# Transposing normalised rows and key features by DMA instead of on TensorE, in a fused attention and feed-forward kernel

## Chip, core and metric

The kernel runs on one core of a Trainium2 chip. The metric is the device time of one execution in microseconds (us). The core has five engines with queues of their own: PE (TensorE; PEld is its weight load), DVE (VectorE), ACT (ScalarE), POOL (GpSimd) and SP (SyncE, which here issues every DMA). Each engine takes its instructions strictly in order, and a wait on a semaphore holds everything behind it on that engine.

## What is computed

One layer on x of 2048 rows by 1024 columns, in bf16: a segmented attention with a compressive memory, and a gated feed-forward, each behind a layer norm and with a residual.

```
xn = layernorm(x)
q, k, v = xn @ wq, xn @ wk, xn @ wv            # 32 heads of 32
phi(t) = where(t > 0, t + 1, exp(t))
for s in range(4):                             # segments of 512 rows
    a_dot = softmax(qs @ ks.T * 32**-0.5 + causal mask) @ vs
    a_mem = (phi(qs) @ M) / (phi(qs) @ z + 1e-6)
    o_s = g * a_mem + (1 - g) * a_dot          # g = sigmoid(beta), per head
    M += phi(ks).T @ vs ;  z += phi(ks).sum(rows)
h = x + concat(o_s) @ wo
hn = layernorm(h)
out = h + (silu(hn @ w1) * (hn @ w3)) @ w2     # 3584 hidden columns
```

## The kernel before

Work is described as a graph of operations, each with an engine (or a choice of two), an estimated cost, a priority class and the buffers that it reads and writes. `Graph.schedule` (L208) lays the graph out by a simulated clock of its own: whenever an engine is free, it takes the ready operation of the lowest class number. What comes out is a fixed order of instructions on each engine, and the semaphore waits that the buffers need; the chip runs that order. A DMA is given a short time on SP, its bytes at `DMA_RATE` on one shared line, and `DMA_FIX` more (L77, L78, L326 to L329). Changing one operation can so change the order of all that follows.

PE contracts over the partition dimension, so rows that are to be multiplied by a weight must first lie with their columns on the partitions. The kernel keeps such transposed tiles for each segment s: `xnT[s]` of the normalised input and `hnT[s]` of the normalised residual, both [128, 8, 512] (eight blocks of 128 columns, 512 rows). The tile `xnT[1]` lies in the buffer `hnT0`, `xnT[2]` in `hnT1`, and `xnT[3]` in the buffer of `xnT[0]` (L521).

- `ln1(s)` (L731) loads four tiles of 128 rows into `xs` (four buffers), normalises each in place (statistics on DVE, the inverse root on POOL, the scaling on DVE at L727), transposes it and puts it in `xnT[s]`.
- `qkv(s)` (L747) streams wq, wk and wv in halves of 1 MB into three `wp` buffers, and makes `qT`, `kT` and `v`, in groups of eight matmuls of 512 columns.
- `memory(s)` (L794), for segments 0 to 2, makes the key features phi(k) for two blocks of heads at a time (`pk`, two buffers), transposes them to `pkn` (two buffers), and multiplies them with v (eight matmuls of 129 columns). The product updates M and z.
- `attention(s)` (L838) runs eight units of four heads: scores (L868), three exponentials on ACT (L883), causal masks on POOL (L888), value products and sums (L921), and the division and mixing on DVE and POOL.
- `wo_stage(s)` (L963), four tiles of 128 rows each: the output projection, the residual with a reload of x (`xr`, one buffer), a store of h to a scratch tensor, the norm into `hn` (one buffer), its transpose into `hnT[s]`.
- `ffn_up` and `ffn_down` (L986, L1017) work on two blocks of 1024 rows. Block 0 uses `hnT[0]` and `hnT[1]`. The output projections of segments 2 and 3 are added between chunks of block 0.

A transpose in this kernel is one batch of eight PE instructions (`transposes`, L605, recorded at L609), each with a 128x128 block as one operand and an identity as the other. The batch claims one bank of the accumulator (PSUM), and `evac` (L616) copies the 128x1024 result to SBUF on DVE (L621) or ACT (L620), whichever the planner finds free. As long as attention runs, dense work has two of the eight banks, 6 and 7 (`dense_group`, L583); afterwards it has them all. Dense matmuls are recorded at L597.

Of the kernel before, what the change touches and what calls it, by code (L numbers as in the profile page):

```python
# [69 lines left out]
class Graph:  # L70
# [126 lines left out]
    def dma(self, out, in_, cls=5, deps=(), eng="sp"):  # L197
        n = 1
        for s in out.shape:
            n *= s  # L200
        o = self.op("sp", 60.0, None, reads=(in_,), writes=(out,), cls=cls, deps=deps,
                    kind="dma")
        o.emit = lambda e, g: [e.dma_start(out, in_)]
        o.bytes = n * SIZE[out.dtype]
        return o


# [244 lines left out]
def dve_ns(n, mode=1):  # L452
    return 150.0 + n / (0.96 * mode)
# [10 lines left out]
class Kernel:  # L464
# [266 lines left out]
    def ln1(self, s):  # L731
        for i in range(4):
            t = 4 * s + i
            x = self.xs[t % 4][:, :]
            self.g.dma(x, self.x2d[t * 128:(t + 1) * 128, :], cls=0 if s == 0 else 2)
            if t == 1:
                self.ln_act(t, x, x)
            else:
                self.ln(t, x, x, 2 if s == 0 else 5)
            gr = self.dense_group() if s else Group([(6,), (7,), (4,), (5,)], safe=True)  # L740
            self.transposes(gr, [(c * 128, self.xs[t % 4][:, c * 128:(c + 1) * 128])
                                 for c in range(8)], 2 if s == 0 else 4)
            out = self.xnT[s][:, :, i * 128:(i + 1) * 128]
            self.evac(gr, out, 1024, lambda b: b.rearrange("p (k n) -> p k n", k=8), cls=1,
                      bf=True)
# [48 lines left out]
    def memory(self, s):  # L794

        p = s % 2
        v = self.v[p]
        for pr in range(4):
            pk = self.pk[pr % 2]
            self.phi(self.kT[p][:, 2 * pr:2 * pr + 2, :], pk[:, :, :], 4)  # L800
            gr = self.dense_group()
            self.transposes(gr, [((a * 4 + kc) * 128, pk[:, a, kc * 128:(kc + 1) * 128])
                                 for a in range(2) for kc in range(4)], 4)
            pkn = self.pkn[pr % 2]
            self.evac(gr, pkn[:, :, :], 1024, lambda b: b.rearrange("p (k n) -> p k n", k=8),
                      cls=3, bf=True)
            gr = self.dense_group()
            items = []
            for a in range(2):
                for kc in range(4):  # L810
                    items.append((lambda gr, a=a: self.bank(gr, 0, 129, 132 * a),
                                  pkn[:, a * 4 + kc, :], v[:, kc, 2 * pr + a, 0:129],
                                  kc == 0, kc == 3, 129))
            self.mms(gr, items, 4, split=8)
            acc = self.Macc[:, 2 * pr:2 * pr + 2, :]

            def upd(e, gr, acc=acc):
                ps = self.bank(gr, 0, 264).rearrange("p (a n) -> p a n", a=2)[:, :, 0:129]
                if s == 0:
                    return [e.tensor_copy(acc, ps)]  # L820
                return [e.tensor_tensor(acc, acc, ps, op=ALU.add)]

            self.g.op("dve", dve_ns(258), upd, reads=[acc] if s else [], writes=[acc], cls=3,
                      group=gr)
            Mb = self.Mbf[p][:, 2 * pr:2 * pr + 2, :]
            am = self.Macc[:, 2 * pr:2 * pr + 2, 0:128]
            bl = self.blk[:, :].unsqueeze(1).to_broadcast([128, 2, 128])
            self.either(lambda e, Mb=Mb, am=am, bl=bl: e.tensor_tensor(Mb, am, bl, op=ALU.mult),
                        256, 2, [am, self.blk[:, :]], [Mb], 4)
            for a in range(2):  # L830
                zs = self.zsel[p][:, 2 * pr + a, :].rearrange(
                    "p (j n) -> p j n", j=4)[:, :, 1:2].rearrange("p j n -> p (j n)")
                z = self.Macc[:, 2 * pr + a, 128:129]
                hm = self.hmask[:, :]
                self.pool_op(lambda e, zs=zs, z=z, hm=hm: e.tensor_scalar(
                    zs, hm, z, None, op0=ALU.mult), 4, [hm, z], [zs], 4)
# [126 lines left out]
    def wo_stage(self, s):  # L963
        oT = self.oT[s % 2]
        for i in range(4):
            t = 4 * s + i
            xr, h, hn = self.xr[0], self.h[t % 2], self.hn[0]
            self.g.dma(xr[:, :], self.x2d[t * 128:(t + 1) * 128, :], cls=2)
            for half in range(2):
                gr = self.dense_group(s >= 2)  # L970
                self.mms(gr, [(lambda gr: self.bank(gr), oT[:, c, i * 128:(i + 1) * 128],
                               self.wo[:, c, half * 512:(half + 1) * 512], c == 0, c == 7, 512)
                              for c in range(8)], 5 if s < 2 else 7)
                hs = h[:, half * 512:(half + 1) * 512]
                xs = xr[:, half * 512:(half + 1) * 512]
                self.g.op("dve", dve_ns(512), lambda e, gr, hs=hs, xs=xs: [e.tensor_tensor(  # L976
                    hs, xs, self.bank(gr), op=ALU.add)], reads=[xs], writes=[hs], cls=3,
                    group=gr)
            self.g.dma(self.hd[t * 128:(t + 1) * 128, :], h[:, :], cls=3)
            self.ln(16 + t, h[:, :], hn[:, :], 4)  # L980
            gr = self.dense_group(s >= 2)
            self.transposes(gr, [(c * 128, hn[:, c * 128:(c + 1) * 128]) for c in range(8)], 3)
            self.evac(gr, self.hnT[s][:, :, i * 128:(i + 1) * 128], 1024,
                      lambda b: b.rearrange("p (k n) -> p k n", k=8), cls=3, bf=True)

    def ffn_up(self, blk, ch):  # L986
        n = self.n_w13
# [139 lines left out]
```

## Time and profile before

| | |
|---|---|
| time, median of 3 runs | 946.5 us (945.31 to 946.81) |
| the profiled execution, its own time | 944.8 us |
| its span, first to last instruction | 943.1 us |
| PE busy | 915.6 us, 97% |
| DVE busy | 434.7 us, 46% |
| ACT busy | 321.6 us, 34% |
| POOL busy | 172.8 us, 18% |
| moved by DMA | 85.83 MB, 91 GB/s on average |

The profile is one execution, recorded instruction by instruction. A group of instructions is named by its line, engine, operation, and what it writes and reads (`pkn<-ps` writes pkn from the accumulator). "Idle before, releaser" is time in which an engine stood ahead of such an instruction, and the instruction whose end freed it. Matmul ends are modelled, so starts are the better measure of how long one takes.

### The profile page before, as it was taken

Reading aid. Unit: us, or ns where it says so; the run is one execution under the profiler, and the core shown is the slowest. Engines: PE = TensorE matmul, PEld = TensorE weight load, DVE = VectorE, ACT = ScalarE, POOL = GpSimd, SP = SyncE. Lnnn points to the kernel's source line nnn. Section 1 sums busy time; section 2 is a strip of 40 time slices with the busy share of each in tenths; the row PEclk is TensorE's granted clock in tenths of the full one; section 3 lists DMA queues with packets and bytes.
Section 4 is the critical chain, followed back from the end, with each engine's and each line's share of the span. In section 5 each row is a group of like instructions: output and inputs, shape, how many; then the busy total and the mean of one; then the engine's idle time right before and its main releaser. Section 6 shows DMA issues by size and latency. Waiting matters only on the chain.

```text
span 943.1 us, 13518 instructions
## 1 busy us (share of the span) xinstructions
PE 915.6 (97%) x5661; PEld 421.3 (45%) x5760; DVE 434.7 (46%) x749; ACT 321.6 (34%) x360; POOL 172.8 (18%) x274
## 2 busy tenths in 40 slices
PE   7999999998999999999999999999999999999998
PEld 3444344443444444444444444444444444444443
DVE  3895638768766766544544321211333343331101
ACT  4877638787677771121121110000111111110000
POOL 2563313563644552000000000000000000000000
PEclk9999999999999999999999999999999999999999
DMA  9532343222331318433343221011332123300110
GB/s 313 190 117 71 105 141 106 90 90 70 112 101 35 91 45 293 129 114 90 101 145 90 73 62 45 28 40 45 90 91 71 50 63 90 90 17 29 45 45 29
DMA packets 103005, 85.83 MB, mean 91 GB/s; under 512 B 3104, under 2 KB 90144, under 8 KB 102944
## 3 DMA queue, kind: packets, MB, share of 16 engines
q1 hardware_dynamic: 102944, 84.95, 29.5%
q8 instruction: 46, 0.75, 0.3%
q14 instruction: 15, 0.12, 0.0%
HBM read 76.55 MB, written 8.39 MB: 90 GB/s over the span
## 4 chain that ended last, share of the span: by engine, by line
PE 94%; ACT 2%; DVE 2%; issue 1%; DMA 1%; SPq 0%; DVEq 0%; ACTq 0%
PE ps L597 86%; PE ps L921 4%; PE ps L868 3%; PE ps L609 1%; DMA xr<-in_A_x_dram 1%; DVE h L976 1%; ACT eB L883 0%; DMA xs<-in_A_x_dram 0%; ACT eA L883 0%; DVE lnst L718 0%; ACT xnT L620 0%; ACT v L620 0%; DVE v L621 0%; ACT qT L620 0%; ACT pkn L620 0%
## 5 line engine op out<-in xcount | busy, mean ns | idle before, releaser
L597 PE MATMUL ps<-hnT,w1b 128*128 128x512 bf16 x875 | 221.0, 379 | 1.4 <-issue 0.3
L597 PE MATMUL ps<-hnT,w3b 128*128 128x512 bf16 x875 | 220.2, 379 | 2.0 <-issue 0.6
L1005 ACT ACTIVATE sg<-ps 128x512 bf16<-128x512 f32 x112 | 66.9, 597 | 407.6 <-PE ps L597 400.4
L597 PE MATMUL ps<-w2b,hm 128*128 128x512 bf16 x880 | 195.5, 379 | 0.8
L1008 DVE SCALAR_TENSOR_TENSOR t<-sg,ps 128x512 bf16<-128x512 bf16 x112 | 76.9, 686 | 158.5 <-ACT sg L1005 158.4
L597 PEld LDWEIGHTS ps<-w2b,hm 128*128 128x128 bf16 x896 | 87.7, 98 | 105.7
L597 PEld LDWEIGHTS ps<-hnT,w3b 128*128 128x128 bf16 x896 | 87.0, 98 | 105.4 <-issue 1.6
L597 PEld LDWEIGHTS ps<-hnT,w1b 128*128 128x128 bf16 x896 | 86.7, 98 | 104.1 <-issue 6.2
L1013 DVE SCALAR_TENSOR_TENSOR hm<-t,ps 128x512 bf16<-128x512 bf16 x112 | 76.9, 686 | 81.1 <-PE ps L597 79.2
L1035 DVE TENSOR_TENSOR ob<-hr,ps 128x512 bf16<-128x512 bf16 x32 | 22.0, 687 | 143.4 <-PE ps L597 143.4
L883 ACT ACTIVATE eA<-ps 128x2048 bf16<-128x2048 f32 x32 | 60.0, 1876 | 15.8 <-PE ps L868 9.4
L597 PE MATMUL ps<-xnT,wp 128*128 128x512 bf16 x244 | 58.4, 379 | 2.9 <-issue 1.6
L597 PE MATMUL ps<-hnT,wp 128*128 128x512 bf16 x246 | 59.1, 380 | 1.4 <-issue 1.3
L597 PE MATMUL ps<-wo,oT 128*128 128x512 bf16 x248 | 58.8, 379 | 1.4 <-DVE h L976 0.6
L888 POOL TENSOR_SCALAR_AFFINE_SELECT eC<-eC 128x512 bf16<-128x512 bf16 x64 | 41.0, 662 | 41.7 <-ACT eC L883 41.7
L883 ACT ACTIVATE eC<-ps 128x1536 bf16<-128x1536 f32 x32 | 46.4, 1450 | 6.2 <-PE ps L868 6.1
L883 ACT ACTIVATE eB<-ps 128x1536 bf16<-128x1536 f32 x32 | 46.3, 1447 | 5.9 <-PE ps L868 5.9
L932 DVE STREAM_TRANSPOSE T<-ps 128x512 f32<-128x512 f32 x32 | 22.9, 716 | 37.0 <-PE ps L921 37.0
L888 POOL TENSOR_SCALAR_AFFINE_SELECT eA<-eA 128x512 bf16<-128x512 bf16 x32 | 21.4, 670 | 89.1 <-ACT eA L883 89.1
L868 PE MATMUL ps<-qT,kT 32*128 32x256 bf16 (+3 forms) x512 | 34.5, 302 | 3.0 <-ACT eB L883 1.2
L597 PEld LDWEIGHTS ps<-wo,oT 128*128 128x128 bf16 x256 | 24.0, 98 | 29.0 <-issue 0.9
L597 PEld LDWEIGHTS ps<-xnT,wp 128*128 128x128 bf16 x256 | 23.1, 98 | 28.5 <-issue 3.7
(108 smaller groups left out, 795.7 us busy)
## 6 DMA issues: line engine op xcount, KB each, us to landing
w1b<-in_B_w_dram SPq DMA_DIRECT2D x28, 512.0 KB, 3.9
w3b<-in_B_w_dram SPq DMA_DIRECT2D x28, 512.0 KB, 3.8
wp<-in_A_wk_dram SPq DMA_DIRECT2D x8, 1024.0 KB, 5.4
wp<-in_A_wv_dram SPq DMA_DIRECT2D x8, 1024.0 KB, 6.0
wp<-in_A_wq_dram SPq DMA_DIRECT2D x7, 1024.0 KB, 5.2
w2b<-in_B_w_dram SPq DMA_DIRECT2D x7, 1024.0 KB, 8.0
xs<-in_A_x_dram SPq DMA_DIRECT2D x16, 256.0 KB, 3.7
xr<-in_A_x_dram SPq DMA_DIRECT2D x16, 256.0 KB, 2.9
```

What stands on the lines that cost most here:

```text
L597: return [e.matmul(p[0](gr), p[1], p[2], start=p[3], stop=p[4]) for p in part]
L609: return [e.transpose(b[:, c:c + 128], s, self.ident[:, :]) for c, s in items]
L868: ins.append(e.matmul(self.bank(gr, j, n, off), k[r, g, 128 * kc:128 * kc + 128], q[r, g, 128 * kc:512], start=True, stop=True, tile_posit ...
L883: return [e.activation(et[:, :, :], src, AF.Exp, scale=self.scale)]
L888: self.pool_op(lambda e, m=m: e.affine_select(m, m, pattern=[[0, 4], [1, 128]], compare_op=ALU.is_ge, fill=0.0, base=0, channel_multiplier ...
L921: ins.append(e.matmul(self.ps[r, b * 512 + 128 * kc:(b + 1) * 512], lhsT, src[:, j, :], start=first, stop=True, tile_position=(0, 32 * j), ...
L932: G.op("dve", dve_ns(512), lambda e, gr: [e.transpose(T1, self.bank(gr))], writes=[T1], cls=0, group=gd)
L976: self.g.op("dve", dve_ns(512), lambda e, gr, hs=hs, xs=xs: [e.tensor_tensor(hs, xs, self.bank(gr), op=ALU.add)], reads=[xs], writes=[hs], ...
L1005: self.g.op("act", act_ns(512), lambda e, gr, sg=sg: [e.activation(sg, self.bank(gr), AF.Tanh, scale=0.5)], writes=[sg], cls=2, group=gg)
L1008: e.scalar_tensor_tensor(t1, sg, 1.0, self.bank(gr), op0=ALU.add, op1=ALU.mult)], reads=[sg], writes=[t1], cls=2,
L1013: e.scalar_tensor_tensor(dst, t1, 0.5, self.bank(gr), op0=ALU.mult, op1=ALU.mult)], reads=[t1], writes=[dst], cls=2,
L1035: self.g.op("dve", dve_ns(512), lambda e, gr, hs=hs, ob=ob: [e.tensor_tensor(ob, hs, self.bank(gr), op=ALU.add)], reads=[hs], writes=[ob], ...
```

## The change

The transposes of three kinds of tiles are no longer made by PE. A new graph operation, `dma_t`, is one DMA on SP that reads a tile of 128 rows by 1024 columns in SBUF and writes it, transposed in blocks of 128 columns, to another place in SBUF. It claims no bank, and nothing is evacuated. It is planned with 2 x 262144 bytes.

```
+    def dma_t(self, out, in_, cls=5):
+        o = self.op("sp", 60.0, None, reads=(in_,), writes=(out,), cls=cls, kind="dma")
+        o.emit = lambda e, g: [e.dma_start_transpose(out, in_)]
+        o.bytes = 2 * 262144
+        return o
...
# ln1
-            gr = self.dense_group() if s else Group([(6,), (7,), (4,), (5,)], safe=True)
+            if s:
+                self.g.dma_t(self.xnT[s][:, :, i * 128:(i + 1) * 128], x, 3)
+                continue
+            gr = Group([(6,), (7,), (4,), (5,)], safe=True)
...
# memory
-            gr = self.dense_group()
-            self.transposes(gr, [((a * 4 + kc) * 128, pk[:, a, kc * 128:(kc + 1) * 128])
-                                 for a in range(2) for kc in range(4)], 4)
             pkn = self.pkn[pr % 2]
-            self.evac(gr, pkn[:, :, :], 1024, lambda b: b.rearrange("p (k n) -> p k n", k=8),
-                      cls=3, bf=True)
+            self.g.dma_t(pkn[:, :, :], pk[:, :, :].rearrange("p a n -> p (a n)"), 3)
...
# wo_stage
-            gr = self.dense_group(s >= 2)
-            self.transposes(gr, [(c * 128, hn[:, c * 128:(c + 1) * 128]) for c in range(8)], 3)
-            self.evac(gr, self.hnT[s][:, :, i * 128:(i + 1) * 128], 1024,
-                      lambda b: b.rearrange("p (k n) -> p k n", k=8), cls=3, bf=True)
+            self.g.dma_t(self.hnT[s][:, :, i * 128:(i + 1) * 128], hn[:, :], 2)
```

The first segment's rows stay on PE. 320 PE instructions and 40 evacuations go, and 40 DMAs come. A tile that such a DMA reads (`xs`, `pk`, `hn`) may be overwritten only when the DMA has finished. All engines' orders are laid out anew, and the lines behind the new function have other numbers (L597 is L604, L868 is L874, L921 is L927).

## The prediction

> **What bounds the kernel now.** I read the profile from the whole to the parts: busy time of each engine, the chain of work that ended last, then stretches of time, then the transposes themselves. From the first page, span, busy time and chain:
>
> ```profile
> span 943.1 us, 13518 instructions
> PE 915.6 (97%) x5661; PEld 421.3 (45%) x5760; DVE 434.7 (46%) x749; ACT 321.6 (34%) x360; POOL 172.8 (18%) x274
> PE 94%; ACT 2%; DVE 2%; issue 1%; DMA 1%; SPq 0%; DVEq 0%; ACTq 0%
> ```
>
> PE is busy for 915.6 of 943.1 us and holds 94% of the chain, so only what shortens PE's own queue, or lengthens what it waits for, can move the end. The busy time by stretches (the columns are PE, its weight loads, DVE, ACT, POOL, the granted clock, the DMA engines' share and GB/s) shows where PE is not busy:
>
> ```profile
> 0.00:15.00 15.00, 9.21 (x56) 4.59 (x58) 7.37 (x23) 6.91 (x9) 7.03 (x25) 1.00 0.91 275
> 15.00:355.00 340.00, 324.69 (x2880) 149.91 (x2922) 232.49 (x428) 244.43 (x238) 154.50 (x229) 1.00 0.33 105
> 355.00:510.00 155.00, 153.68 (x775) 72.08 (x789) 78.87 (x129) 29.12 (x44) 11.32 (x20) 1.00 0.46 138
> ```
>
> From 15 to 355 us (projections, attention, and dense work between) PE idles 15.3 us, ACT is busy for 244 of 340 us, DVE for 232, the DMA engines for a third. After 355 us PE has hardly a gap. The clock is 1.00 throughout, so no term below needs a correction for it.
>
> **What is removed on PE.** The same view for L609, the line of all transposes, PE and weight loads:
>
> ```profile
> 0.00:15.00 15.00, 2.21 (x32) 1.81 (x32) 1.00 0.91 275
> 15.00:943.00 928.00, 24.32 (x320) 19.39 (x320) 1.00 0.29 88
> ```
>
> The 32 before 15 us are the first segment's and stay. The other 320, in 40 batches of eight, go: 12 for rows of segments 1 to 3, 12 for key features, 16 for the rows after the output projection. The rows are 24.32 us busy, 0.61 us a batch, but the end of a matmul is modelled and the next one starts before it. The timeline of PE gives the step from one start to the next:
>
> ```profile
> 35.87 0.62 PE L609 MATMUL ps<-ident,pk 128*128 128x128 bf16 x8
> 36.45 0.62 PE L609 MATMUL ps<-ident,xs 128*128 128x128 bf16 x8
> 37.28 0.63 PE L597 MATMUL ps<-v,pkn 128*128 128x129 bf16 x8 [0.21 <-DVE pkn L621]
> ...
> 79.76 0.61 PE L609 MATMUL ps<-ident,pk 128*128 128x128 bf16 x8
> 80.30 0.40 PE L921 MATMUL ps<-eA,v 128*32 128x512 bf16 x4
> ...
> 103.39 0.62 PE L609 MATMUL ps<-ident,pk 128*128 128x128 bf16 x8
> 103.85 0.38 PE L597 MATMUL ps<-wp,hnT 128*128 128x512 bf16 x1
> ```
>
> The steps are 0.58 (36.45 less 35.87), 0.54 and 0.46 us; between 0.46 and 0.61 I take 0.55, nearest to the middle one. 40 x 0.55 = 22 us, with bounds 18.4 and 24.3. The chain passes through PE nearly everywhere, so this comes off the end, not only off a busy sum.
>
> **What goes with it.** A batch also holds one of two accumulator banks until it is evacuated. What PE waited for from 15 to 355 us, with the sum, the number and the longest:
>
> ```profile
> PE ps L609 <- DVE h L976: 1.4, 1, 1.4
> PE ps L609 <- DVE v L621: 0.7, 2, 0.3
> PE ps L597 <- ACT xnT L620: 0.6, 1, 0.6
> PE ps L609 <- ACT v L620: 0.5, 2, 0.2
> PE ps L597 <- DVE pkn L621: 0.2, 1, 0.2
> PE ps L597 <- ACT pkn L620: 0.2, 1, 0.2
> ```
>
> The three waits on xnT and pkn (1.0 us) go, since nothing is evacuated there. The waits of the transposes on v and h (2.6 us) were for a bank that some other matmul will now want: I count them as staying. So 1 us, between 0 and 3.6.
>
> The 40 evacuations leave ACT and DVE. The 23 and 17 of them take 1.02 and 0.69 us each by the pkn groups (ACT, DVE):
>
> ```profile
> L620 ACT ACTIVATE pkn<-ps 128x1024 bf16<-128x1024 bf16 x5 | 5.1, 1022 | 2.7 <-PE ps L609 2.7
> L621 DVE COPY pkn<-ps 128x1024 bf16<-128x1024 bf16 x7 | 4.8, 688 | 0.9 <-PE ps L609 0.6
> ```
>
> That is 23 us of ACT and 12 us of DVE, worth nothing directly, since both have a third of the stretch free; they only make late evacuations less likely.
>
> **What is added.** 40 crossbar transfers of 256 KB, issued by SP in order with the weight loads. No row shows such a transfer. The nearest are plain DMAs (KB each, us from issue to landing):
>
> ```profile
> xr<-in_A_x_dram SPq DMA_DIRECT2D x16, 256.0 KB, 2.9
> xs<-in_A_x_dram SPq DMA_DIRECT2D x16, 256.0 KB, 3.7
> wp<-in_A_wv_dram SPq DMA_DIRECT2D x8, 1024.0 KB, 6.0
> w2b<-in_B_w_dram SPq DMA_DIRECT2D x7, 1024.0 KB, 8.0
> wo<-in_A_wo_dram SPq DMA_DIRECT2D x1, 2048.0 KB, 11.6
> ```
>
> Bounds: 2.9 us, a transfer of the same size that is merely copied, and 11.6 us, the longest landing on the page. I take 4 us, near the rows of equal size, with a little for the transposing. [...]
>
> Who waits for it, in order of how soon? The tightest consumer is the memory product of key features (L597, v and pkn). PE's order there, first segment, before; pk is the key-feature tile, pkn its transpose, the L868 rows are score products:
>
> ```order
> L597 MATMUL ps<-wp_76,xnT 128x512 x12
> L868 MATMUL ps<-qT_82,kT_83 128x384 x4
> L609 MATMUL ps<-ident,pk_90 128x128 x8
> L609 MATMUL ps<-ident,xs_77 128x128 x8
> L597 MATMUL ps<-v_84,pkn_94 128x129 x8
> ```
>
> And the same place in PE's queue after (L927 is what was L921, the value products):
>
> ```order
> L604 MATMUL ps<-wp_76,xnT 128x512 x12
> L874 MATMUL ps<-qT_82,kT_83 128x384 x4
> L604 MATMUL ps<-xnT,wp_74 128x512 x12
> L874 MATMUL ps<-qT_82,kT_83 128x256 x4
> L874 MATMUL ps<-qT_82,kT_83 128x128 x4
> L927 MATMUL ps<-eA_96,v_84 32x512 x4
> ...
> L604 MATMUL ps<-xnT,wp_74 128x512 x4
> L874 MATMUL ps<-qT_82,kT_83 128x512 x4
> L604 MATMUL ps<-v_84,pkn_94 128x129 x8
> ```
>
> The product has moved back by 16 projection matmuls and one unit's value products. Their steps on PE before, and the end of the pk tile on DVE:
>
> ```profile
> 29.88 2.76 PE L597 MATMUL ps<-wp,xnT 128*128 128x512 bf16 x12
> 32.58 0.40 PE L868 MATMUL ps<-qT,kT 32*128 32x512 bf16 x4
> ...
> 38.11 0.40 PE L921 MATMUL ps<-eA,v 128*32 128x512 bf16 x4
> 39.54 0.81 PE L597 MATMUL ps<-xnT,wp 128*128 128x512 bf16 x3 [0.16 <-issue]
> ...
> 34.70 0.64 DVE L791 TENSOR_TENSOR pk<-phe,phr 128x1024 bf16<-128x1024 bf16 x1
> ```
>
> 12 matmuls step 2.70 us (32.58 less 29.88), so 16 take 3.6; the value products step 1.43 (39.54 less 38.11); two score batches, each below the 0.40 of the quoted row since ends overlap, about 0.6: 5.6 us after 35.87, so 41.5. pk is done at 35.34. That leaves 6.1 us from ready to wanted, and a landing of 4 us fits. There are 12 such places; for those where the transfer stands behind a 1 MB load I keep 2 us in all, between 0 and what the slow rival below gives.
>
> The other 28 have more room. SP's queue at the same place, before (wp are projection weights, xs rows of the input):
>
> ```order
> L203 DMA wp_75<-in_A_wk_dram 128x8x512
> L203 DMA wp_76<-in_A_wv_dram 128x8x512
> L203 DMA xs_77<-in_A_x_dram 128x1024
> L203 DMA xs_78<-in_A_x_dram 128x1024
> L203 DMA xs_79<-in_A_x_dram 128x1024
> L203 DMA xs_80<-in_A_x_dram 128x1024
> L203 DMA wp_74<-in_A_wq_dram 128x8x512
> ```
>
> And after (hnT_72 takes the transposed rows of segment 1):
>
> ```order
> L203 DMA wp_75<-in_A_wk_dram 128x8x512
> L210 DMA_TRANSPOSE pkn_94<-pk_90 128x8x128
> L203 DMA wp_76<-in_A_wv_dram 128x8x512
> L210 DMA_TRANSPOSE hnT_72<-xs_77 128x8x128
> L210 DMA_TRANSPOSE pkn_95<-pk_91 128x8x128
> L210 DMA_TRANSPOSE hnT_72<-xs_78 128x8x128
> L210 DMA_TRANSPOSE hnT_72<-xs_79 128x8x128
> L210 DMA_TRANSPOSE hnT_72<-xs_80 128x8x128
> L203 DMA xs_77<-in_A_x_dram 128x1024
> L203 DMA wp_74<-in_A_wq_dram 128x8x512
> ```
>
> Six transposes have come in between. They wait for DVE's tiles, and the load of wp_74 for segment 1 is queued behind them and behind a reload of xs_77 that needs a finished transpose. The cover is the lead of that load: issued here, first used there (SP, then PE):
>
> ```profile
> 54.48 0.38 SPq L203 DMA_DIRECT2D wp<-in_A_wq_dram  x1
> 81.73 0.59 PE L597 MATMUL ps<-hnT,wp 128*128 128x512 bf16 x2 [0.16 <-issue]
> ```
>
> 27 us ahead, with a landing of 6.0 us by the wp row: SP may be some 20 us late before PE notices. I count nothing. Without that cover each microsecond of lateness would be one of PE.
>
> Last, the single hn buffer: a new row may be written only when the transfer has read the old one, and DVE waits with its evacuations queued behind. Two hn rows before stand at:
>
> ```profile
> 142.93 0.54 DVE L727 TENSOR_SCALAR hn<-h,lnmv,rstd 128x1024 bf16<-128x1024 bf16 x1
> 146.38 0.54 DVE L727 TENSOR_SCALAR hn<-h,lnmv,rstd 128x1024 bf16<-128x1024 bf16 x1
> ```
>
> 3.45 us apart, against 4 us: at most half a microsecond of DVE, which has a third of its time free. Nothing on the path.
>
> Sum, against the profiled execution's own 944.8 us (span 943.1 and 1.7 around it): 944.8 - 22 - 1 + 2 = 923.8. The median of the runs before, 946.5, is 1.7 above that execution; a median of runs after should stand likewise, so I give 925.5. About 0.2% is what a measurement here can tell from no change, 944.6 to 948.4.
>
> **The rivals.**
>
> Forecast (0.68): as above. With the outer values of each gain, 24.3 and 3.6 instead of 22 and 1, and no new wait, it is 946.5 - 27.9 = 918.6; a denser order by the shorter evacuation queues could add some of the other idle time, a third of 15.3 us, so 913.5.
>
> The time saved turns into idle time (0.12): attention could be held by its exponentials on ACT, and PE would wait for scores instead of transposing. For it: ACT is the next busiest engine there, with 244 of 340 us. Against it: ACT has 96 us free from 15 to 355 us and loses 23 more of work, and feed-forward matmuls fill in. If half the gain is lost, 946.5 - 11 = 935.5.
>
> The crossbar lands late (0.15, slower): the eight 128-column blocks of a transfer pass one after the other, and PE stands at the 12 products of pkn. At the landing of the w2b row, 8.0 us, each lacks 2 us, 24 in all: 946.5 - 23 + 24 = 947.5; at 11.6 us each lacks 5.6, 67 in all, and it is 990. It decides from 6 + 23/12 = 7.9 us on. For it: nothing here shows 128 columns turned by a DMA, and SP puts five transfers in a row, which would then also queue. Against it: rows of equal size land in 2.9 to 3.7 us. [...]
>
> Little or no change (0.05): the two last in part, by a landing of about 7.9 us.
>
> That the change doesn't do what it says is excluded by the order: of L609's 44 batches PE keeps the first four.
>
> **The numbers.** Range 913.5 to 949: the forecast's best end, the idle rival, and the late crossbar to its near end; beyond it lie the late crossbar's long end, about 0.12, and a little below. Faster by over 0.2%: 0.68 + 0.12 = 0.80; within: 0.05; slower: 0.15.
>
> **What would show it.** Right: transposing DMAs landing in 3 to 5 us, PE busy about 892 us, idle from 15 us on about as before, no row of PE waiting on pkn over 1 us. Wrong: landings above 8 us, PE waits on pkn, hnT or wp that add up to over 10 us, or DVE waiting on hn's transfer with evacuations late behind it.

## The result and the profile after

The changed kernel takes 916.8 us (median of 4 runs, 916.1 to 919.0) against 945.9 us before: ratio 0.9697, 95% interval 0.9676 to 0.9719, some 29 us less. The forecast was 925.5 us, with a range down to 913.5.

The profiled execution took 916.63 us. Its span, busy times and chain, from the first page:

```profile
span 914.6 us, 12864 instructions
PE 895.2 (98%) x5346; PEld 402.7 (44%) x5440; DVE 431.8 (47%) x739; ACT 295.2 (32%) x330; POOL 173.5 (19%) x274
PE 95%; DVE 2%; issue 1%; ACT 1%; DMA 0%; POOL 0%; SPq 0%; ACTq 0%
```

PE is still the bound, busy for 98% of the span and with 95% of the chain. Of the 28.5 us that the span lost, PE's busy time gave 20.4 (915.6 less 895.2) and its idle time 8.1 (27.5 to 19.4). Both traces miss about as many matmul records (94 of 5440 here, 99 of 5760 before), so the difference can be used. The idle time of one trace alone is overstated: the trace of the section "What a new order is worth" below, whose order is mostly that of before, misses none of 5760 and shows 17.9 us idle in a span of 942.9. Neither it nor the other traces below that miss none (the plans with 1, 3 and 8 tiles) has a row "issue" for PE from 15 to 330 us; so such rows are holes that missing records leave, not waits. ACT lost 26 us and 30 instructions: 23 evacuations, and seven others that the new order puts on DVE.

Where the idle time went can be read from the busy time by stretches and from what PE waited for, here from 15 to 330 us:

```profile
15.00:330.00 315.00, 307.81 (x2594) 135.06 (x2632) 228.73 (x415) 221.04 (x213) 150.87 (x224) 1.00 0.53 142
```

```profile
PE ps L604 <- issue: 4.6, 29, 0.2
PE ps L604 <- DVE h L982: 0.7, 2, 0.5
PE ps L604 <- DVE qT L628: 0.4, 1, 0.4
PE ps L604 <- DVE kT L628: 0.3, 1, 0.3
PE ps L604 <- DVE T L943: 0.2, 1, 0.2
PE ps L604 <- DVE lnst L725: 0.2, 1, 0.2
```

Apart from "issue", 1.8 us of waits are left. In the trace of before the same table, over the same stretch, has 8.7 us in thirteen rows. Not only the waits on xnT and pkn are gone, but also those of the transposes on h and v, of other dense matmuls on h, and the waits on exponentials and reciprocals. Of before, beside the rows that the prediction shows:

```profile
PE ps L597 <- DVE h L976: 1.2, 2, 0.6
PE ps L868 <- ACT eA L883: 1.1, 1, 1.1
PE ps L597 <- DVE o L952: 0.9, 1, 0.9
PE ps L868 <- ACT eB L883: 0.8, 2, 0.5
PE ps L868 <- DVE Rc L941: 0.6, 1, 0.6
```

The new transfers, from the page and the list of DMA issues (KB each where known, median us from issue to landing):

```profile
q1 hardware_dynamic: 145184, 95.45, 37.9%
...
xs<-in_A_x_dram SPq DMA_DIRECT2D x16, 256.0 KB, 6.9
...
hnT<-hn SPq DMA_TRANSPOSE x16, 3.9
pkn<-pk SPq DMA_TRANSPOSE x12, 3.6
hnT<-xs SPq DMA_TRANSPOSE x8, 3.5
xnT<-xs SPq DMA_TRANSPOSE x4, 3.2
```

They land in 3.2 to 3.9 us, close to the 4 us of the forecast. The input rows, reloaded behind them in the same queue, now land in 6.9 us where they took 3.7; in the other orders below that have all 40 transfers it is between 3.5 and 6.0, so much of that is this order's.

The first memory product, whose slack the prediction worked out. SP's queue and PE's timeline (start, length):

```profile
35.58 1.34 SPq L210 DMA_TRANSPOSE pkn<-pk  x1
36.98 0.56 SPq L203 DMA_DIRECT2D wp<-in_A_wv_dram  x1
37.58 2.63 SPq L210 DMA_TRANSPOSE hnT<-xs  x1
40.26 2.71 SPq L210 DMA_TRANSPOSE pkn<-pk  x1
43.01 4.67 SPq L210 DMA_TRANSPOSE hnT<-xs  x3
47.73 0.58 SPq L203 DMA_DIRECT2D xs<-in_A_x_dram  x1
48.35 0.44 SPq L203 DMA_DIRECT2D wp<-in_A_wq_dram  x1
```

```profile
36.09 2.76 PE L604 MATMUL ps<-xnT,wp 128*128 128x512 bf16 x12
38.79 0.34 PE L874 MATMUL ps<-qT,kT 32*128 32x256 bf16 x8
...
41.56 0.63 PE L604 MATMUL ps<-v,pkn 128*128 128x129 bf16 x8
```

The product starts at 41.56, without a wait in front of it (41.5 was worked out), 6 us after SP issued its transfer. The five transfers that SP issues from 37.58 on hold it for some 10 us, yet the load of wq behind them leaves at 48.35, earlier than before (54.48).

### The profile page after: what moved, and what is told of

The parts are those of the page before. It is cut to its first block, busy times and chain, and to the rows that moved or that the text cites. A ratio compares the mean times of both kernels' runs of the same rounds, so it can differ in the third digit from the quotient of the medians.

```text
span 914.6 us, 12864 instructions
## 1 busy us (share of the span) xinstructions
PE 895.2 (98%) x5346; PEld 402.7 (44%) x5440; DVE 431.8 (47%) x739; ACT 295.2 (32%) x330; POOL 173.5 (19%) x274
## 3 DMA queue, kind: packets, MB, share of 16 engines
q1 hardware_dynamic: 145184, 95.45, 37.9%
## 4 chain that ended last, share of the span: by engine, by line
PE 95%; DVE 2%; issue 1%; ACT 1%; DMA 0%; POOL 0%; SPq 0%; ACTq 0%
PE ps L604 88%; PE ps L927 4%; PE ps L874 3%; DMA xs<-in_A_x_dram 0%; DVE lnst L725 0%; DVE h L982 0%; DVE t L1011 0%; DVE hm L1016 0%; ACT eA L889 0%; ACT sg L1008 0%; PE ps L616 0%; ACT eB L889 0%; DVE T L938 0%; ACT xnT L627 0%; DVE xs L734 0%
## 5 line engine op out<-in xcount | busy, mean ns | idle before, releaser
L604 PE MATMUL ps<-hnT,w1b 128*128 128x512 bf16 x877 | 220.6, 379 | 1.4 <-issue 0.6
L604 PE MATMUL ps<-hnT,w3b 128*128 128x512 bf16 x877 | 220.2, 379 | 1.3 <-issue 0.5
L604 PE MATMUL ps<-w2b,hm 128*128 128x512 bf16 x878 | 195.4, 379 | 0.9
L604 PEld LDWEIGHTS ps<-w2b,hm 128*128 128x128 bf16 x896 | 87.6, 98 | 105.8
L604 PEld LDWEIGHTS ps<-hnT,w3b 128*128 128x128 bf16 x896 | 87.0, 98 | 104.8 <-issue 0.9
L604 PEld LDWEIGHTS ps<-hnT,w1b 128*128 128x128 bf16 x896 | 87.0, 98 | 104.4 <-issue 5.5
L604 PE MATMUL ps<-xnT,wp 128*128 128x512 bf16 x246 | 59.4, 380 | 3.7 <-issue 1.3
L604 PE MATMUL ps<-hnT,wp 128*128 128x512 bf16 x248 | 59.4, 380 | 1.5 <-issue 0.8
L604 PE MATMUL ps<-wo,oT 128*128 128x512 bf16 x247 | 58.3, 379 | 1.1 <-issue 0.6
L604 PEld LDWEIGHTS ps<-wo,oT 128*128 128x128 bf16 x256 | 23.9, 98 | 28.9 <-issue 2.1
L604 PEld LDWEIGHTS ps<-xnT,wp 128*128 128x128 bf16 x256 | 22.9, 98 | 30.4 <-issue 3.9
L604 PEld LDWEIGHTS ps<-hnT,wp 128*128 128x128 bf16 x256 | 23.4, 98 | 28.9 <-issue 2.6
L874 PE MATMUL ps<-qT,kT 32*128 32x256 bf16 (+3 forms) x512 | 34.5, 302 | 0.4 <-ACT eB L889 0.3
```

Of the source, the lines that this page charges most:

```text
L604: return [e.matmul(p[0](gr), p[1], p[2], start=p[3], stop=p[4]) for p in part]
L874: ins.append(e.matmul(self.bank(gr, j, n, off), k[r, g, 128 * kc:128 * kc + 128], q[r, g, 128 * kc:512], start=True, stop=True, tile_posit ...
```

## Experiments

**The theory (A):** TensorE is the bound, so each batch that leaves it takes its own work off the end, and with it the waits that it and its evacuation cause; the gain is a sum over batches. **Rival B:** what exceeds PE's own work came from the new order that the planner happened to lay out. **A second rival** is the late crossbar of the prediction, which must then be seen when it is provoked. All ratios are to the kernel before, measured again beside each group of runs (medians 947.0 to 947.6 us), so runs are best compared by their ratios.

### One kind of tile at a time

Each kernel keeps the new operation for one kind of tile and takes the old code for the two others, for instance:

```
# rows of segments 1 to 3 only: memory and wo_stage as before
...
-            self.g.dma_t(pkn[:, :, :], pk[:, :, :].rearrange("p a n -> p (a n)"), 3)
+            self.evac(gr, pkn[:, :, :], 1024, lambda b: b.rearrange("p (k n) -> p k n", k=8),
+                      cls=3, bf=True)
...
-            self.g.dma_t(self.hnT[s][:, :, i * 128:(i + 1) * 128], hn[:, :], 2)
+            self.transposes(gr, [(c * 128, hn[:, c * 128:(c + 1) * 128]) for c in range(8)], 3)
```

> Only the 12 batches of normalised input rows (segments 1 to 3) go by DMA; key features and the rows behind the output projection stay on TensorE. Theory A (each batch takes its own work and its waits off TensorE, so the parts add): 29 us over 40 batches is 0.73 us a batch, so 12 x 0.73 = 9 us, about 937 where before is 946. Rival B (what exceeds TensorE's own 0.51 us a batch came from the new order as a whole, laid out once): the work alone, 12 x 0.51 = 6 us, about 940, and the three parts do not add up to the whole gain.

> Only the 12 batches of key features go by DMA. Theory A: 12 x 0.73 = 9 us, about 937, with landings near 3.6 us and no wait of TensorE on pkn above 1 us. Rival B: about 940. If the transfers were late for their product (the late crossbar of the prediction), this part alone would be no faster than before.

> Only the 16 batches of rows behind the output projection go by DMA. Theory A: 16 x 0.73 = 12 us, about 934; if the waits belong to the two banks that dense work has while attention runs, the 8 batches of segments 2 and 3, made later with all banks free, give only 0.51 us each, and it is 946 - 8 x 0.73 - 8 x 0.51 = 936. Rival B: 16 x 0.51 = 8 us, about 938.

| by DMA | us | ratio, 95% interval | gain | PE idle in the trace (span less busy), us |
|---|---|---|---|---|
| none (before) | | | | 27.5 |
| input rows, 12 | 937.0 | 0.9897 (0.9875 to 0.9919) | 1.03% | 23.7 |
| key features, 12 | 935.6 | 0.9886 (0.9865 to 0.9908) | 1.14% | 23.9 |
| rows behind the projection, 16 | 936.6 | 0.9896 (0.9872 to 0.9919) | 1.04% | 26.1 |
| all 40 | 916.8 | 0.9697 (0.9676 to 0.9719) | 3.03% | 19.4 |

The three sum to 3.21%; together they gave 3.03% (2.81 to 3.24). They add, as theory A has it, and so does PE's idle time: it falls by 3.8, 3.6 and 1.4 us, 8.8 together, against 8.1 for all 40 (each trace misses 94 to 99 records). Each part has an order of its own, so a gain that belonged to one lucky order would not be expected to add. Key features, the tiles with the tightest consumer, gain as much as the others, though their transfers landed in 4.7 us and not in the expected 3.6; no row of PE names them. The 16 rows behind the projection gain less per batch (0.065% against 0.09%), which fits that half of them are made when dense work has more than two banks. The intervals are too wide to show it; the idle time, which hardly falls there, points the same way.

### TensorE's work given back

Beside each of the 40 transfers the old batch is run as well, into a bank that nobody reads; the data still comes by DMA. One of the three places:

```
+            gr = self.dense_group()
+            self.transposes(gr, [(c * 128, x[:, c * 128:(c + 1) * 128]) for c in range(8)], 4)
```

> The changed kernel, and beside each of the 40 transposing DMAs the old batch of eight TensorE transposes of the same tile as well, into a bank that nobody reads: TensorE's work is back, the evacuations are not, and the data still comes by DMA. Theory A: 20 us of work come back, a little with them for banks: 937 to 939. If banks and evacuations account for nothing and only the order gained, 937 too, so this run prices the work alone; if TensorE's work were hidden after all, it stays near 917.

Measured: 939.5 us, 0.9928 (0.9902 to 0.9954). 2.31% of the 3.03% is back, 22 us, half a microsecond above the expected range. In the trace PE's busy time is back (914.4 us, 19.2 above the change), and of the idle time only 2.5 us (21.9, against 19.4 in the change and 27.5 before). So TensorE's own work is most of the gain. The waits that grew are not for banks in the main; the largest row from 15 to 330 us is score products waiting for exponentials:

```profile
PE ps L879 <- ACT eB L894: 2.8, 2, 1.6
```

### And the evacuations

The same, and each batch is read and rewritten in its bank before the bank is free.

```
+            if e is self.nc.scalar:
+                return [e.activation(v, v, AF.Copy)
+                        for v in (self.bank(gr, 0, 172), self.bank(gr, 0, 172, 172),
+                                  self.bank(gr, 0, 168, 344))]
+            return [e.tensor_copy(self.bank(gr), self.bank(gr))]
```

> As the run before it with the TensorE batches back, and each batch is also read and written back in place in its bank by DVE or ACT, as the planner chooses (one DVE copy of 512 float32, or three ACT copies that make up 512), before the bank is free: work, bank hold and evacuations are back, only the data still comes by DMA. Theory A (work 20 us, banks and evacuations 8 us): 944 to 947, all of the gain gone. Rival B (the 8 us came from the new order or from the data not waiting for evacuations): it stays at 937 to 940.

Measured: 943.3 us, 0.9956 (0.9941 to 0.9972), below the expected 944 to 947 and above the rival's 937 to 940. PE now waits on the evacuations themselves, 2.2 us from 15 to 330 us (L636 and L639 are the copies put back):

```profile
PE ps L604 <- DVE ps L639: 1.2, 3, 0.5
PE ps L604 <- ACT ps L636: 1.0, 1, 1.0
```

That is 0.28% more than without the evacuations, with overlapping intervals, so the price of the evacuations is not shown by the times alone. PE's idle time is 24.6 us, 2.7 above the run without them and 2.9 below before; each figure is from one execution. 0.44% (0.28 to 0.59), some 4 us, is still missing to the kernel before. Neither theory alone has that: it may be consumers no longer standing behind an evacuation, or the order.

### What a new order is worth

The kernel before, with nothing moved, but the planner told that a transpose takes longer:

```
-        o = self.g.op("pe", len(items) * 66.0, emit,
+        o = self.g.op("pe", len(items) * 76.0, emit,
```

> The kernel before, with nothing moved off TensorE, but the planner told that a transpose takes 76 ns instead of 66, which lays the order out anew. It measures what a new order is worth by itself. Theory A: within 3 us of before, 943 to 949. Rival B (the 8 us beyond TensorE's own work came from a new order): it can move by 5 us or more.

Measured: 947.1 us, 1.0002 (0.9987 to 1.0017): nothing. This new order brought no gain. But most of PE's order is the same as before, and the next runs show that other orders do cost, so it doesn't exclude rival B for the last 4 us.

### What the planner believes of a transfer

The DMAs are unchanged; only the bytes with which the planner reckons differ, from an eighth of the changed kernel's to four times as many. At the planner's 260 bytes per ns and 1.9 us more (L77, L78) the five sizes of the table below mean planned landings of 2.2, 2.9, 3.9, 4.9 and 10.0 us.

```
-        o.bytes = 2 * 262144
+        o.bytes = 262144 // 4      # and 262144, 3 * 262144, 8 * 262144
```

> The changed kernel, planned as if a transposing DMA moved an eighth of the bytes; the DMAs themselves are the same. The planner then puts consumers about 2 us sooner behind the transfer. Theory A (the order leaves the transfers just room enough, and their landing of 3.2 to 3.9 us counts once it is undercut): waits of TensorE on pkn appear, up to 1.5 us at 12 places, 917 to 930. Rival (there is room to spare): 917.

> The changed kernel, planned with half the bytes for each transposing DMA (their true size); an eighth of the bytes had cost 13 us. Theory A (the order must leave the transfers about their landing of 3.2 to 3.9 us and their place in SP's queue): consumers come 1 us sooner than in the changed kernel, some waits on pkn return, 917 to 924. Rival B (the order as such, by chance, makes the difference): anywhere within some 10 us of 917, either way.

> The changed kernel, planned with half as many bytes again (three times the true size). Theory A: once transfers land in time, more room buys nothing: 915 to 919. Rival B: anywhere within some 10 us of 917.

> The changed kernel, planned with eight times the true bytes, about 10 us for a transfer alone. Theory A: consumers stand far behind, so no wait on a transfer; the price can only be in memory updates and normalised rows that come late for what follows, and in weight loads issued otherwise: 915 to 925. Rival B: anywhere within some 10 us of 917.

| planned bytes, in tiles of 262144 | us | ratio, 95% interval |
|---|---|---|
| 1/4 | 930.4 | 0.9829 (0.9805 to 0.9852) |
| 1 | 921.5 | 0.9736 (0.9712 to 0.9760) |
| 2 (the change) | 916.8 | 0.9697 (0.9676 to 0.9719) |
| 3 | 926.6 | 0.9788 (0.9766 to 0.9810) |
| 8 | 993.9 | 1.0505 (1.0478 to 1.0532) |

The short side came out as expected in size, but not as a dozen small waits. With a quarter, the worst stand of PE (a stretch in which it waits) is at a memory product. SP's queue before it, and there the weight load (PEld) and the matmul (PE):

```profile
65.68 5.60 SPq L210 DMA_TRANSPOSE hnT<-xs  x4
71.32 2.17 SPq L203 DMA_DIRECT2D xs<-in_A_x_dram  x4
73.53 1.24 SPq L210 DMA_TRANSPOSE pkn<-pk  x1
```

```profile
78.52 0.79 PEld L604 LDWEIGHTS ps<-v,pkn 128*128 128x128 bf16 x8 [4.78 <-DMA pkn<-pk]
78.53 1.05 PE L604 MATMUL ps<-v,pkn 128*128 128x129 bf16 x8 [4.61 <-DVE lnst L725]
```

The matmul names a DVE instruction that happened to end there; the weight load names the transfer, which was issued behind four transposes and four reloads and landed some 5 us later. A second stand, 3.04 us at 49.5 us, goes back to the reloads of x: DVE, in its fixed order, waits for one, and only then frees the bank that PE needs:

```profile
50.77 0.69 DVE L725 BATCH_NORM_STATS2 lnst<-xs 128x6 f32<-128x512 bf16 x1 [5.89 <-DMA xs<-in_A_x_dram]
...
52.54 2.75 PE L604 MATMUL ps<-xnT,wp 128*128 128x512 bf16 x12 [3.04 <-DVE Macc L826]
```

With one tile the waits on pkn were 0.5 us in all, too little for the 4 us lost (0.39% by the ratios, whose intervals just overlap); the rows there show waits for exponentials instead, and why they came is open.

On the long side the expectation failed. With 3 the worst gap of PE is 4.71 us at 111 us, for a bank that DVE frees only after a run of normalisations in its queue:

```profile
115.95 1.02 PE L604 MATMUL ps<-v,pkn 128*128 128x129 bf16 x8 [4.71 <-DVE h L982]
```

That accounts for half of the 10 us, the matmuls at a lower clock behind it (last section) for some 2 more; the rest is spread. With 8, a transfer takes 8.1 us of the planner's one line, so that it thinks the rows of segment 1 late and lays their projections far back; the attention of segment 0 then runs without dense work in between. One of PE's waits there, and one stretch:

```profile
79.71 0.51 PE L874 MATMUL ps<-qT,kT 32*128 32x256 bf16 x8 [1.56 <-ACT eB L889]
```

```profile
80.00:120.00 40.00, 22.26 (x152) 10.00 (x144) 19.68 (x39) 6.23 (x4) 11.84 (x25) 0.64 0.16 42
```

Between 80 and 120 us PE is busy for 22 of 40 us and its clock is at 0.64. None of these planned sizes beats the change. Only with a quarter was a loss traced to transfers; each size is one order, so a best planned landing is not shown.

### The late crossbar, made on purpose

Each transfer of key features is cut into eight of one 128x128 block:

```
-            self.g.dma_t(pkn[:, :, :], pk[:, :, :].rearrange("p a n -> p (a n)"), 3)
+            for a in range(2):
+                for kc in range(4):
+                    self.g.dma_t(pkn[:, a * 4 + kc:a * 4 + kc + 1, :],
+                                 pk[:, a, kc * 128:(kc + 1) * 128], 3, 8)
```

> The changed kernel with each transfer of key features cut into eight transposing DMAs of one 128x128 block, planned with an eighth of the bytes each. SP held 1.24 us for a whole transfer when nothing stood before it; if a block holds it as long, eight take 10 us, and the product stands some 7 us late at 12 places: up to 85 us, at least 30, so 947 to 1000. If only bytes count, 917 to 922. This is the late crossbar of the prediction made on purpose, and prices it.

Measured: 990.2 us, 1.0458 (1.0430 to 1.0486), as expected of the late crossbar. SP's queue at the first two tiles, what PE waited for in all, and the landing of one block:

```profile
35.58 1.19 SPq L210 DMA_TRANSPOSE pkn<-pk  x1
36.83 0.56 SPq L203 DMA_DIRECT2D wp<-in_A_wv_dram  x1
37.43 9.49 SPq L210 DMA_TRANSPOSE pkn<-pk  x7
46.97 1.31 SPq L210 DMA_TRANSPOSE hnT<-xs  x1
48.32 10.16 SPq L210 DMA_TRANSPOSE pkn<-pk  x8
```

```profile
PE ps L604 <- DMA pkn<-pk: 56.6, 10, 10.9
```

```profile
pkn<-pk SPq DMA_TRANSPOSE x96, 2.4
```

A block holds SP for 1.2 us (the median) and lands in 2.4, eight in a row take over 10, and PE stands 56.6 us at ten products. The span grew by 75 us (914.6 to 989.6); most of the other 18 is matmuls at a lower clock after such a stand: PE's busy time is 911.8 us, 16.6 above the change, and its clock 0.90 on average from 15 to 330 us.

### The first segment as well

```
-            if s:
-                self.g.dma_t(self.xnT[s][:, :, i * 128:(i + 1) * 128], x, 3)
-                continue
...
+            self.g.dma_t(self.xnT[s][:, :, i * 128:(i + 1) * 128], x, 3 if s else 0)
```

> The changed kernel with the first segment's four row tiles by DMA too. Those batches start the kernel: TensorE waits for the first tile anyway, and the first projection stands behind the last. Theory A: 2 us of TensorE work go, but a transfer has to get past 2 to 3 MB of weights in the same queue, so it lands in 6 to 9 us where batch and evacuation took 2: 920 to 926. Rival (transposing by DMA is better wherever it is put): 915.

Measured: 931.2 us, 0.9833 (0.9819 to 0.9848), 14 us more than the change (13 by the ratios) and worse than expected. SP and PE at the start, PE's first projection in the change for comparison, and two stretches of this run with the granted clock as the figure before the last two:

```profile
11.36 13.66 SPq L210 DMA_TRANSPOSE xnT<-xs  x4
```

```profile
23.46 8.07 PE L604 MATMUL ps<-wp,xnT 128*128 128x512 bf16 x24 [16.70 <-DMA xnT<-xs]
```

```profile
13.30 10.60 PE L604 MATMUL ps<-xnT,wp 128*128 128x512 bf16 x47 [1.21 <-ACT xnT L627]
```

```profile
20.00:25.00 5.00, 1.54 (x4) 0.58 (x5) 0.00 (x0) 0.00 (x0) 0.00 (x0) 0.50 1.16 268
25.00:30.00 5.00, 5.00 (x15) 1.86 (x14) 1.82 (x4) 0.76 (x2) 0.00 (x0) 0.60 0.94 262
```

Behind the weights the four transfers hold SP 13.66 us, PE waits 16.7 us, and the first matmuls then run at 0.50 to 0.60 of the clock. The first projection starts 10 us later than in the change (23.46 against 13.30), and its first 24 matmuls take 8.07 us, where 47 take 10.60 in the change. Nothing covers a transfer here.

## Why the prediction was right, and what was mis-sized

The direction and the mechanism were right, the size was 8 us short (21 forecast, 29 measured), inside the range. In the terms of its sum, 22 + 1 - 2 = 21 us became 20.4 of busy time, 8.1 of idle time and no new wait on a transfer, 28.5. By its steps:

- **TensorE's work, 22 us.** Busy time fell by 20.4 us, and giving the batches back brought 19.2 us of it back, with 2.5 us more of idle time. Right.
- **Waits that go, 1 us, between 0 and 3.6.** This is the step that failed. The prediction counted only rows that named a transposed tile, and let the waits on h and v stay "for a bank that some other matmul will now want". PE's waits apart from "issue" fell from 8.7 to 1.8 us. No other matmul took these waits over. The evacuations put back brought waits on DVE and ACT back, so part of it belongs to them; for some 4 us of the gain the runs don't tell consumers freed of an evacuation from the order. The prediction also named idle time "about as before" as a sign of being right; it fell, so that sign did not come. Its 15.3 us of idle time held the holes of missing records too.
- **New waits at pkn, 2 us.** None: the median landing was 3.6 us (the longest 7.0), the slack at the first place 6. The slack was worked out to 41.5 and came to 41.56, in part by luck: the 1.43 us for the value products holds one matmul whose record is missing (1.21 us in the trace that misses none), and PE reached its 12 projection matmuls 0.2 us later than assumed (36.09, not 35.87).
- **A landing of 4 us.** 3.2 to 3.9. Right, and the eight blocks of a transfer don't pass one after the other at the price of a block: alone one lands in 2.4 us (median, the run with blocks), eight together in 3.6 (median of pkn), so an estimated (3.6 - 2.4) / 7 = 0.17 us for each further one. Eight transfers of a block each held SP for 10.16 us.
- **SP's queue costs nothing.** Right for the weight loads: no row of PE from 15 to 330 us names wp. The xs reloads became slower in this order, 6.9 us instead of 3.7, which the prediction didn't price; in the order of the change no row of PE names them. In that of the quarter plan a transfer of pkn was late behind four reloads and four transposes, and DVE's 5.89 us for a reload cost PE 3.04.
- **The hn buffer.** DVE waited once on a transfer of hn, 1.1 us, off the path. Right.
- **The rivals.** Saved time did not turn into idle time; idle time fell. The late crossbar was a real danger with about the price given (67 us at 12 places forecast for a landing of 11.6, 56.6 measured at ten for a little over 10), but lower clocks add to it, which the prediction left out.

## What to carry to other kernels

Here one engine was the bound (PE, 97% of the span) and DMA had room (a share of 0.33 from 15 to 355 us), and work that a transfer could do beside PE was worth its full step there, an estimated half a microsecond a batch (20.4 us over 40). It was worth over a third more, 28.5 us of span: its results no longer pass through banks and evacuations, and for some 4 us the order may have helped. So price the waits of the neighbours as well, not only those that name the removed tile.

It held only while something else filled the landing: with the first segment's rows by DMA nothing did, and PE waited 16.7 us. Move whole tiles, not blocks (1.23 to 2.78 us of SP for a pkn tile whole, 10.16 for one in blocks), and leave a transpose on the engine where the engine has nothing else to do. If a planner sets the order, vary the landing that it reckons with: the change was planned with 3.9 us, about what was measured, and both shorter and longer ones lost 5 to 77 us here, though not all of that through the transfers.

## What the runs showed of the hardware

**After long stands TensorE ran at a lower clock.** After the 4.71 us gap in the plan with 3 tiles, the granted clock was 0.50 for the next matmuls:

```profile
116.00:120.00 4.00, 4.00 (x16) 1.95 (x17) 2.04 (x5) 0.00 (x0) 1.94 (x5) 0.50 0.76 195
```

There the output projection's weight loads start 0.43 us apart (117.20, 117.62), where 12 projection matmuls of 512 columns step 2.70 us at a clock of 1.00, 0.225 each; four microseconds at about half that rate are another 2 us lost, by estimate. In the run with blocks the seven stands of 4.1 us and more were each followed by a memory product of 1.02 or 1.03 us; after the three of up to 2.6 us it took 0.61. It was seen after short waits that lay close, too: in the plan with 8, four waits of 0.4 to 1.6 us between 68 and 75.4 us left PE busy for half of 70 to 76 us, and from 76 to 82 us the clock was at 0.50 (the sums of eA step 0.43 us at 75.76, where they stepped 0.22 at 70.70). In the change, no gap of PE from 15 to 330 us is longer than 0.5 us by the table above, and the clock stays at 1.00 there.

**A transposing DMA took more of the DMA engines than a copy.** The queue's share rose from 29.5% of 943.1 us to 37.9% of 914.6, 278 to 347 us, for 40 transfers: 1.71 us of all engines for 262 KB, 153 GB/s, where the plain transfers of before made 84.95 MB in 278 us, 305 GB/s. That counts the whole rise against the transfers, also what they may add to the packet times of their neighbours. In the plan with 8 one transfer moves alone, and in the kernel before one reload of x with one store of h (the last three figures are the clock, the share and GB/s):

```profile
110.00:112.00 2.00, 0.00 (x0) 0.00 (x0) 2.00 (x6) 0.00 (x0) 0.79 (x2) 0.50 0.69 131
113.50:117.00 3.50, 3.19 (x17) 1.09 (x15) 1.94 (x5) 0.00 (x0) 1.89 (x4) 1.00 0.53 150
```

The transfer has 0.69 of 2 us, 1.38 us of all engines or 190 GB/s, the two plain ones 0.53 of 3.5 us, 283 GB/s. So a transfer had half to two thirds of a plain DMA's rate (153 against 305 GB/s, 190 against 283). In the change a transfer held SP for 1.23 us or more; in the kernel before, a plain DMA that SP issued after at least half a microsecond of rest held it for 0.32 to 0.39. With the DMA engines' share at 0.53 from 15 to 330 us, no row of PE named a DMA in the order of the change.
